# A long convolution and a SwiGLU on one core: another order of the steps in all five queues

## The chip, the cores and the metric

The kernel runs on one core of a Trainium2 chip. The metric is the device time of one execution in microseconds (us). Four engines compute: TensorE (PE, matmuls), VectorE (DVE), ScalarE (ACT) and GpSimd (POOL); SyncE (SP) issues nearly all transfers. Each engine works through its own list of instructions in order, and waits on semaphores where a step needs the result of another engine or of a transfer.

## The reference

For one sequence of S = 2048 rows with D = 640 channels in bf16 (F = 1728):

```python
def _A_ref(q, k, v, shift_k, ssm_k, ssm_D):       # q: a layernorm of A_q
    k_shift = sum over t of k_pad[:, t:t + S, :] * shift_k[:, ks - 1 - t]     # 4 taps
    kv = k_shift * v
    y_f = rfft(kv, padded to 2 S) * rfft(ssm_k, padded to 2 S)
    y = irfft(y_f)[:S] + kv * ssm_D
    return q * y

def _B_ref(x, w_gate, w_up, w_down):
    return (silu(x @ w_gate) * (x @ w_up)) @ w_down

x = A_q
h = x + _A_ref(_layernorm(x), A_k, A_v, A_shift_k, A_ssm_k, A_ssm_D)
h2 = h + _B_ref(_layernorm(h), B_w_gate, B_w_up, B_w_down)
```

(The first lines are shortened in their writing, not in what they compute.)

## The kernel before

**Blocks and stages.** The sequence is cut into four blocks of 512 rows, numbered 0 to 3. The long convolution is done block by block through a half-shifted discrete Fourier transform of 512 points, written as matmuls with a table of cosines and sines. The names below are those of the code, with i for the block:

- *k filter* (kt0 to kt3, kf0 to kf3). kc is the load of a block of ssm_k; kt transposes it on TensorE (line 538), ACT copies it to KT (L543); kf transforms it with the table ftab (matmuls L582, eviction to C and KO by ACT L595, butterflies by DVE L552), and DVE adds neighbouring blocks (L666). kf1 to kf3 each have eight matmul steps of four matmuls.
- *kv* (kv1 to kv3). kT is a transposing load of k's block (L484), of which PE makes the shifted sum of four taps (L686, L691) in three steps; ACT evicts them (L715; L698 in block 0); for blocks 1 to 3 five transposing transfers turn the result back into kvo (the "kvt pieces", L484), and three DVE products multiply v into it (L724, vt). In block 0 PE transposes back instead.
- *ln* (L784 to L813). Statistics and scaling of the gate, q; x is its load, L813 the scaling.
- *xf*, *p*, *iv*. The transform of kv, the products of block j's transform with the filter's (DVE, L753, L754, L759, L769), and the inverse transform with the table itab (PE, L830).
- *hn* (L850 to L889). DVE multiplies the inverse by q, ACT and POOL take the second LayerNorm's statistics, ACT scales (L886; in block 0 DVE, L889), and four transposing transfers per block, the "hn pieces", write hnT.
- *ff* (L911 to L988). Gate and up matmuls (L911, L912; L922 for the last half block), SiLU and copy on ACT (L934, L936), product on DVE (L938), down matmuls (L954, L966), eviction (ACT L974 with DVE L981; DVE L984 in block 3), and the store of the output (out, L988). Weights: GA, UA, GB, UB, PK, Wd.

**The order of work.** Every step is a task, numbered in the order in which the program creates it. `ORDER` is a table of these numbers, one list for each engine, and says in which order an engine's queue holds its tasks. `_Graph.schedule` replays the lists with a planner's costs. It assigns the accumulators (PSUM, four units of two banks each) in the order in which that replay reaches the tasks, so that a task also waits until the last users of its unit are done. It also counts filler: where the replay finds PE idle for more than 700 ns ahead of a step that opens a unit, `t.fill` throwaway matmuls of about 83 ns are put ahead of it (L249). `emit` then writes each engine's instructions with the waits that the dependences require.

```python
                if self.warm is not None and e == "pe" and at[e] > 2:
                    idle = s - max(free[e], unit_free[u])
                    t.fill = int((idle - 250) / 83) if idle > 700 else 0
```

Two helpers issue nearly all transfers: `load` (L479, a plain DMA) and `tload` (L484, a transposing DMA), both on SP except for a few loads at the start.

**The numbers used in the text.**

| queue | steps |
|---|---|
| SP | loads: 0 ident, 3 ftab, 4 itab, 17 kc0, 57 kc1, 62 kc2, 67 kc3; 19 v0, 314 v1, 507 v2, 710 v3; 138 x0, 312 x1, 505 x2, 708 x3; 225 UA, 224 GA, 227 UB, 226 GB, 228 and 229 PK, 230 to 233 Wd |
| SP | transposing: 18 kT0, 313 kT1, 506 kT2, 709 kT3; kvt1 317, 318, 321, 322, 325; kvt2 510, 511, 514, 515, 518; kvt3 713, 714, 717, 718, 721; hn0 202, 209, 216, 223; hn1 399, 408, 417, 426; hn2 602, 611, 620, 629; hn3 814, 823, 832, 841 |
| SP | stores: out0 298, 302, 307, 311; out1 491, 495, 500, 504; out2 694, 698, 703, 707; out3 905, 908, 912, 915 |
| PE | kt1 58, 60; kt2 63, 65; kt3 68, 70; kf1 72 to 86, kf2 94 to 108, kf3 114 to 128 (even numbers); kv1 315, 319, 323; kv2 508, 512, 516; kv3 711, 715, 719; iv0 192 to 195; ff0 from 238; ff1's down steps 486, 487, 488, 492, 496, 497, 501; ff2 from 630 |
| ACT | for a PE step n of kt, kf or kv, step n + 1 is its eviction (95 for 94, 123 for 122, 712, 716 and 720 for kv3); 156 to 159 the scaling in ln0; 198 an eviction of iv0; 619 the last scaling ahead of the hn2 pieces |
| DVE | 132 the first butterfly of kf3 that needs 123; 519 to 521 the products of kv2, 722 to 724 those of kv3; 777, 779 and 780 three steps in the products of the filter with blocks 1 and 2 (about 1.4, 1.4 and 0.7 us in the planner's costs) |

Of the kernel before, what the change touches and what calls it, by code (L numbers as in the profile page):

```python
# [58 lines left out]
class _Graph:  # L59
# [170 lines left out]
    def emit(self, block):  # L230
# [75 lines left out]

ORDER = {
    "pe": """
# [6 lines left out]
    """,  # L315
    "act": """
# [12 lines left out]
    """,  # L329
    "dve": """  # L330
# [10 lines left out]
    """,  # L341
    "pool": """
        5 10 6 8 7 9 11 153 197 218 204 200 211 221 207 214 338 423 405 396 414 531 626 608 599 617 734 838 820 829 811
    """,
    "sp": """
# [3 lines left out]
    """,  # L349
}  # L350

# [716 lines left out]
```

## Time and profile before

| | |
|---|---|
| median of 3 runs | 273.35 us (273.2 to 273.37) |
| span of the profiled execution | 269.5 us; its own time outside the span isn't recorded |
| median less span | 3.85 us |
| busy in the span: PE | 255.2 us (95%), 1643 instructions |
| busy in the span: DVE | 203.8 us (76%), 282 instructions |
| busy in the span: ACT | 206.9 us (77%), 394 instructions |
| busy in the span: POOL | 24.1 us (9%), 35 instructions |
| moved by DMA | 25.85 MB |

The span runs from the first to the last recorded instruction of one execution; the times are the device times of separate executions. Busy time counts an engine's instructions alone, so that issuing a DMA or waiting on a semaphore is idle time there. Several rows below come from views that group instructions: "x20" is the number in the group, and "[2.01 <-DMA kT]" at the end of a row says that the engine had been idle for 2.01 us before it and that a transfer into kT ended that.

### The profile page before, as it was taken

The page shows a single profiled execution, that of the slowest core. Times are in us where ns is not written, and L with a number is a line of the kernel's source. Part 1 is how long each engine was busy: PE and PEld are TensorE (multiplying, and loading weights), DVE is VectorE, ACT ScalarE, POOL GpSimd, SP SyncE. Part 2 cuts the span into 40 slices and gives each one's busy share as a digit, 9 for nine tenths or more (in the row PEclk, how much of TensorE's full clock was granted, in tenths as well). Part 3 has the DMA queues.
Part 4 walks back from the last instruction along what each step waited for, and adds up shares of the span by engine and source line. Part 5 has one row for each costly group of instructions (what it writes and reads, how often), then busy time and mean ns, then how long its engine had stood idle before and what let it go on. Part 6 is the DMA issues. An engine that isn't in the chain of part 4 may idle for free.

```text
span 269.5 us, 4198 instructions
## 1 busy us (share of the span) xinstructions
PE 255.2 (95%) x1643; PEld 144.2 (53%) x1660; DVE 203.8 (76%) x282; ACT 206.9 (77%) x394; POOL 24.1 (9%) x35
## 2 busy tenths in 40 slices
PE   7799797999999999999999997999999999999995
PEld 5576455545444666554446574454446674444663
DVE  2399999899999999999999998999996100042312
ACT  2799999797889999479969997399889963647400
POOL 0000315000030013000200141000200200000000
PEclk9999999999999999999999999999999999999999
DMA  6999909551173608643000336510000050010002
GB/s 124 373 355 369 340 19 124 112 138 73 30 261 122 103 0 103 135 155 100 0 1 16 86 63 119 129 80 1 2 0 0 2 122 0 2 49 0 0 27 99
DMA packets 42501, 25.85 MB, mean 96 GB/s; under 512 B 32241, under 2 KB 41202, under 8 KB 42482
## 3 DMA queue, kind: packets, MB, share of 16 engines
q1 hardware_dynamic: 41824, 25.58, 35.7%
q8 instruction: 13, 0.21, 0.3%
q10 hardware_dynamic: 658, 0.01, 0.1%
q14 instruction: 6, 0.05, 0.1%
HBM read 15.69 MB, written 2.62 MB: 68 GB/s over the span
## 4 chain that ended last, share of the span: by engine, by line
DVE 41%; PE 27%; ACT 19%; DMA 6%; SPq 3%; issue 2%; POOL 1%; DVEq 0%
PE ps L954 11%; DVE T L753 6%; DVE T L754 6%; PE ps L912 6%; PE ps L911 5%; DVE T L759 5%; DVE Y L769 5%; DVE gu L938 4%; DVE X L552 3%; SPq L484 3%; DMA kT<-in_A_k_dram 3%; ACT KT L543 3%; ACT KO L595 2%; DVE C L666 2%; DMA kc<-in_A_ssm_k_dram 2%
## 5 line engine op out<-in xcount | busy, mean ns | idle before, releaser
L954 PE MATMUL ps<-Wd,gu 128*128 128x384 bf16 (+1 forms) x416 | 59.0, 299 | 0.2 <-ACT qo L854 0.2
L912 PE MATMUL ps<-hnT,UA 128*128 128x512 bf16 x140 | 53.1, 379 | 0.5
L911 PE MATMUL ps<-hnT,GA 128*128 128x512 bf16 x132 | 50.0, 379 | 1.3 <-DMA hnT<-qo 1.3
L954 PEld LDWEIGHTS ps<-Wd,gu 128*128 128x128 bf16 x416 | 40.0, 98 | 18.3 <-issue 1.3
L936 ACT ACTIVATE ub<-ps 128x512 bf16<-128x512 f32 (+1 forms) x60 | 33.7, 568 | 18.5 <-PE ps L912 11.3
L912 PE MATMUL ps<-hnT,UB 128*128 128x512 bf16 x120 | 45.5, 379 | 0.2
L911 PE MATMUL ps<-hnT,GB 128*128 128x512 bf16 x117 | 44.3, 379 | 0.0
L938 DVE TENSOR_TENSOR gu<-gu,ub 128x512 bf16<-128x512 bf16 x52 | 21.5, 421 | 25.1 <-ACT ub L936 13.2
L934 ACT ACTIVATE gu<-ps 128x512 bf16<-128x512 f32 x52 | 29.8, 596 | 12.6 <-PE ps L912 12.4
L753 DVE TENSOR_TENSOR T<-X,C 128x2560 bf16<-128x2560 bf16 x20 | 29.7, 1486 | 0.2
L754 DVE TENSOR_TENSOR T<-X,C 128x2560 bf16<-128x2560 bf16 x20 | 29.7, 1486 | 0.1
L911 PEld LDWEIGHTS ps<-hnT,GA 128*128 128x128 bf16 x140 | 13.7, 98 | 18.2 <-DMA hnT<-qo 1.9
L582 PE MATMUL ps<-KT,ftab 128*128 128x320 bf16 x128 | 19.9, 300 | 2.5 <-ACT KT L543 1.8
L912 PEld LDWEIGHTS ps<-hnT,UA 128*128 128x128 bf16 x140 | 13.7, 98 | 15.7
L881 POOL TENSOR_TENSOR mv<-mv,half 128x1 f32<-128x1 f32 x16 | 13.7, 859 | 68.2 <-ACT mv L874 68.2
L911 PEld LDWEIGHTS ps<-hnT,GB 128*128 128x128 bf16 x120 | 11.7, 98 | 14.2 <-ACT ub L936 0.2
L759 DVE TENSOR_TENSOR T<-T 128x1280 bf16<-128x1280 bf16 x24 | 19.2, 819 | 0.1
L912 PEld LDWEIGHTS ps<-hnT,UB 128*128 128x128 bf16 x120 | 11.7, 98 | 14.0
L582 PE MATMUL ps<-vt,ftab 128*128 128x320 bf16 x128 | 19.0, 299 | 0.1
L804 POOL TENSOR_TENSOR st<-st,half 128x8 f32<-128x8 f32 x4 | 7.9, 1981 | 113.1 <-ACT st L798 113.1
L769 DVE TENSOR_TENSOR Y<-Y,T 128x2560 bf16<-128x2560 bf16 x12 | 17.8, 1484 | 0.0
L582 PEld LDWEIGHTS ps<-KT,ftab 128*128 128x128 bf16 x128 | 11.0, 98 | 10.7 <-ACT KT L543 3.1
(86 smaller groups left out, 376.5 us busy)
## 6 DMA issues: line engine op xcount, KB each, us to landing
kc<-in_A_ssm_k_dram SPq DMA_DIRECT2D x4, 640.0 KB, 10.1
vt<-in_A_v_dram SPq DMA_DIRECT2D x4, 640.0 KB, 4.8
xh<-in_A_q_dram SPq DMA_DIRECT2D x4, 640.0 KB, 5.9
out_dram<-xh SPq DMA_DIRECT2D x16, 160.0 KB, 2.0
Wd<-in_B_w_down_dram SPq DMA_DIRECT2D x1, 1280.0 KB, 7.5
UA<-in_B_w_up_dram SPq DMA_DIRECT2D x1, 1120.0 KB, 13.5
GA<-in_B_w_gate_dram SPq DMA_DIRECT2D x1, 1120.0 KB, 10.5
UB<-in_B_w_up_dram SPq DMA_DIRECT2D x1, 960.0 KB, 7.5
```

What stands on the lines that cost most here:

```text
L582: last = e.matmul(pt.f(c, W), ftab[:, cs, j, f * P:(f + 1) * P], src[:, j, c * W:(c + 1) * W], start=(j == par), stop=(j == par + 2))
L753: g.add("dve", nm, lambda e, x=x, k=k, t1=t1: e.tensor_tensor(out=t1, in0=x, in1=k, op=ALU.mult), cdve(2560), r=[x, k], w=[t1])
L754: g.add("dve", nm, lambda e, x=x, k=ksw, t2=t2: e.tensor_tensor(out=t2, in0=x, in1=k, op=ALU.mult), cdve(2560), r=[x, k], w=[t2])
L759: g.add("dve", nm, lambda e, p=p, q=q, d=d, op=op: e.tensor_tensor(out=d, in0=p, in1=q, op=op), cdve(1280), r=[p, q], w=[d])
L769: g.add("dve", nm, lambda e, y=y, z=z: e.tensor_tensor(out=y, in0=y, in1=z, op=ALU.add), cdve(2560), r=[y, z], w=[y])
L881: g.add("pool", nm, lambda e, m=m: e.tensor_tensor(out=m[:, 3:4], in0=m[:, 2:3], in1=half[:, 1, 0:1], op=ALU.pow), 650, r=[m[:, 2:3], half ...
L911: e.matmul(pt.f(0, N), wg[:, c, f0:f0 + P], hnT[:, c, :], start=(c == 0), stop=(c == NC5 - 1))
L912: last = e.matmul(pt.f(1, N), wu[:, c, f0:f0 + P], hnT[:, c, :], start=(c == 0), stop=(c == NC5 - 1))
L934: g.add("act", nm, lambda e, pt=pt, gv=gv, a=ps_g, ts=ts: e.activation(out=gv, in_=pt.f(a[0], N, a[1])[:, ts], func=ACTF.Silu, scale=gain) ...
L936: g.add("act", nm, lambda e, pt=pt, uv=uv, a=ps_u, ts=ts: e.activation(out=uv, in_=pt.f(a[0], N, a[1])[:, ts], func=ACTF.Copy, scale=gain) ...
L938: g.add("dve", nm, lambda e, uv=uv, gv=gv: e.tensor_tensor(out=gv, in0=gv, in1=uv, op=ALU.mult), cdve(n), r=[gv, uv], w=[gv])
L954: last = e.matmul(pt.flat(c1 - c0, P + c0), slots[fb][:, j * P:(j + 1) * P], Wd[:, fb, c0:c1], start=(fb == 0 and not second), stop=(fb == ...
```

## The change

All five lists of `ORDER` are replaced. Each holds the same tasks as before; no task is added, removed or altered, and nothing else in the program is touched. What follows from the lists, the units of PSUM, the waits and the filler, is worked out anew by `schedule` and `emit`. Cut to the parts spoken of in this document:

```diff
     "pe": """
-        13 20 24 32 22 35 26 28 39 47 43 37 41 30 51 45 49 170 162 164 166 160 60 172 58 168 174 82 72 80 65 70 63 86 74 68 78 120
-        118 84 124 116 114 128 76 192 193 195 194 126 108 96 319 122 104 315 323 94 102 98 100 106 238 234 246 349 351 357 347 345
...
+        13 20 24 32 22 35 26 28 39 47 43 37 41 30 51 45 49 170 162 160 164 166 60 168 70 172 58 174 65 78 118 76 120 80 68 84
+        82 74 86 114 63 72 124 116 192 195 193 194 108 98 128 94 102 315 319 96 126 122 323 100 106 104 238 234 246 351 347
...
-        439 548 540 538 546 544 542 550 552 431 443 447 451 455 467 463 459 471 475 479 593 591 590 592 486 711 487 488 715 496
-        492 497 719 501 630 638 634 754 762 748 752 758 760 750 756 642 650 646 658 662 654 666 682 670 674 678 805 803 689 804
+        308 516 435 427 439 548 540 538 546 544 542 552 550 431 443 451 447 463 459 455 467 475 471 479 593 591 592 590 486
+        719 715 487 488 496 492 497 711 501 630 638 634 762 752 748 750 754 756 758 642 760 646 662 650 654 658 666 682 674
...
     "act": """
-        85 119 117 125 129 156 157 115 159 158 198 77 199 219 220 205 212 206 213 109 97 127 320 105 123 316 324 103 99 329 95 101
+        75 87 115 64 85 73 125 156 159 157 117 158 198 219 199 205 220 129 206 212 95 99 109 213 316 320 103 97 123 127 101
...
-        465 536 473 469 472 476 535 477 480 481 621 603 534 623 605 483 594 624 484 625 606 612 712 627 607 596 614 597 609 598
-        610 615 628 489 600 616 601 716 618 619 498 720 493 502 632 631 640 639 635 755 636 763 749 759 753 725 761 751 726 757
+        530 461 460 464 456 457 535 536 468 469 465 537 477 534 476 473 480 621 472 603 623 624 594 481 625 612 484 596 597 627
+        483 614 720 598 605 615 716 616 600 606 628 607 489 618 601 609 610 619 493 712 502 498 632 631 639 640 636 763 635
...
     "dve": """
-        186 187 154 188 189 155 191 184 190 90 196 91 130 217 203 210 88 201 131 222 89 208 93 215 92 132 366 365 368 367 327 370
+        186 184 188 187 185 189 154 191 155 190 88 196 90 217 203 130 210 89 201 91 222 92 208 131 215 93 366 365 368 367 327
+        132 328 241 370 326 110 372 369 249 111 361 371 112 362 133 237 374 373 113 375 376 245 363 257 253 364 377 340 380
...
-        746 595 485 747 613 768 770 769 773 771 775 772 490 774 778 499 494 776 724 777 723 503 779 633 722 780 781 783 782 641
+        474 744 604 743 482 595 745 613 746 485 768 747 770 769 773 771 775 772 490 774 778 494 776 780 777 499 779 503 633
+        722 723 724 781 783 782 637 785 784 641 764 786 645 787 765 766 649 788 789 790 767 791 795 653 792 657 661 796 735
...
     "pool": """
-        5 10 6 8 7 9 11 153 197 218 204 200 211 221 207 214 338 423 405 396 414 531 626 608 599 617 734 838 820 829 811
+        5 8 10 9 11 6 7 153 197 218 204 200 211 221 207 214 338 423 405 396 414 531 626 599 617 608 734 838 820 829 811
     "sp": """
-        0 18 17 19 3 138 4 57 225 228 67 62 312 314 232 227 229 224 233 313 202 223 209 216 322 318 325 321 317 226 507 230 231
-        506 426 511 510 408 399 417 514 302 515 518 307 298 311 505 710 709 714 611 713 629 602 491 620 718 500 717 495 721 504
-        708 841 823 832 814 703 698 694 905 908 912 707 915
+        0 18 17 19 3 138 62 229 57 67 232 227 4 228 312 225 224 314 313 202 223 209 216 322 318 317 325 321 226 230 233 231
+        506 426 510 408 399 417 507 511 515 518 514 298 307 302 311 505 709 718 710 629 602 611 620 717 713 714 721 491 504
+        500 495 708 841 823 832 814 698 703 707 912 908 905 694 915
```

38 rows, old and new, of the table ORDER are left out of this document.

## The prediction

> **What bounds the kernel now.** First the head of the page and the table of stretches, whose columns after the stretch's length are the busy time of TensorE (PE), its weight loads (PEld), VectorE (DVE), ScalarE (ACT) and GpSimd (POOL).
>
> ```profile
> span 269.5 us, 4198 instructions
> PE 255.2 (95%) x1643; PEld 144.2 (53%) x1660; DVE 203.8 (76%) x282; ACT 206.9 (77%) x394; POOL 24.1 (9%) x35
> q8 instruction: 13, 0.21, 0.3%
> DVE 41%; PE 27%; ACT 19%; DMA 6%; SPq 3%; issue 2%; POOL 1%; DVEq 0%
> ...
> 13.70:41.00 27.30, 24.93 (x210) 16.33 (x208) 26.66 (x43) 27.22 (x41) 3.07 (x2) 1.00 0.80 264
> 60.00:167.00 107.00, 105.67 (x660) 58.53 (x667) 105.95 (x136) 93.64 (x187) 12.94 (x10) 1.00 0.35 88
> 169.00:204.00 35.00, 34.84 (x178) 17.34 (x180) 34.70 (x45) 28.75 (x57) 1.78 (x1) 1.00 0.13 40
> 204.00:266.30 62.30, 61.92 (x375) 35.26 (x376) 13.77 (x30) 33.26 (x69) 2.20 (x4) 1.00 0.11 30
> ```
>
> PE is busy 95% of the span, yet the chain that ended last runs more through DVE. The table says why. From 13.7 to 41 us ACT is full (27.22 of 27.30). From 60 to 167 and from 169 to 204 DVE and PE are both full, and after 204 PE alone. So there is little to win inside the long stretches; what an order can win are the holes between them. Second, the holes themselves, in the timelines of PE and of DVE; the bracket at the end of a row is the idle time before it and who ended it.
>
> ```profile
> 43.85 1.81 PE L249 MATMUL ps<-ident 128*128 128x192 bf16 x20
> 47.67 1.06 PE L691 MATMUL ps<-kT,dg 64*64 64x512 bf16 x16 [2.01 <-DMA kT<-in_A_k_dram]
> 162.86 0.81 PE L686 MATMUL ps<-kT,dl 128*128 128x512 bf16 x3 [0.61 <-ACT kT L715]
> 168.53 0.39 PE L911 MATMUL ps<-hnT,GA 128*128 128x512 bf16 x1 [1.33 <-DMA hnT<-qo]
> ...
> 46.76 0.45 DVE L889 TENSOR_SCALAR qo<-xh,mv 128x640 bf16<-128x640 bf16 x1 [0.44 <-POOL mv L881]
> 51.29 0.83 DVE L552 TENSOR_TENSOR C<-C,KO 128x1280 bf16<-128x1280 bf16 x1 [0.81 <-ACT C L595]
> 58.72 0.42 DVE L938 TENSOR_TENSOR gu<-gu,ub 128x512 bf16<-128x512 bf16 x1 [0.47 <-ACT ub L936]
> 168.95 0.43 DVE L724 TENSOR_TENSOR vt<-vt,kvo 128x512 bf16<-128x512 bf16 x1 [1.67 <-issue]
> ```
>
> There are two places. Around 44 to 48 us PE does 1.81 us of filler (L249) and waits another 2.01 for kT1, the transposing load of k's second block. Around 167 us PE waits 1.33 us for hnT, the last transposed piece of the third block, and DVE 1.67 us for a product of kv3, whose releaser the profile can't name. Both wait for transposing transfers. Third, then, the transfers in short stretches: the last number of a row is the time from issue to landing, and the GB/s line cuts its stretch, here 40.6 to 47.7 us, in 40 slices of 0.18 us. The five transfer rows below it are of stretches from 40, 146, 164, 214.5 and 165.2 us, the last two of one from 168.
>
> ```profile
> GB/s 0 0 0 0 0 0 0 42 153 131 221 147 185 281 275 274 294 284 293 332 275 271 215 62 10 7 9 48 161 173 190 192 136 13 7 9 9 10 50 112
> ...
> q8 instruction: 1, 0.02, 0.9%
> q14 instruction: 1, 0.01, 0.4%
> ...
> kT<-in_A_k_dram SPq DMA_TRANSPOSE x1, 7.0
> ...
> kT<-in_A_k_dram SPq DMA_TRANSPOSE x1, 4.8
> ...
> hnT<-qo SPq DMA_TRANSPOSE x1, 4.4
> ...
> hnT<-qo SPq DMA_TRANSPOSE x4, 2.6
> ...
> kvo<-kT SPq DMA_TRANSPOSE x1, 3.5
> ...
> out_dram<-xh SPq DMA_DIRECT2D x1, 160.0 KB, 2.0
> kvo<-kT SPq DMA_TRANSPOSE x1, 2.4
> ```
>
> kT1 (40.6) took 7.0 us where kT3 (146.2) took 4.8; the hnT piece that PE waits for (164.1) took 4.4 where the four from 214.9 took 2.6; the kvo piece that DVE waits for (165.4) took 3.5, one at 168.4 took 2.4. In kT1's stretch the packets all but stop twice, for about 0.7 us each, and just two instruction fetches fall into it, one on PE's queue (q8) and one on q14. So a fetch costs transposing transfers in flight some 1 to 2 us. This is what the change goes for.
>
> **Part 1, the start (13 to 60 us).** Every queue holds the same steps in another order, so engine time stays and only waits (and PE's filler) can change. ACT is full from 13.7 to 41 and exchanges steps of equal cost, so step 156, the first LayerNorm scaling, comes at about 37.1 as before: no gain there. UB's load (227) now stands sixth after x0 on SP. It waits until kc1 has been transposed (step 58, by its place at about 23.5 us), and itab, PK, x1, UA, GA, v1 and kT1 wait behind it.
>
> ```profile
> GB/s 124 373 355 369 340 19 124 112 138 73 30 261 122 103 0 103 135 155 100 0 1 16 86 63 119 129 80 1 2 0 0 2 122 0 2 49 0 0 27 99
> ...
> vt<-in_A_v_dram SPq DMA_DIRECT2D x1, 640.0 KB, 4.0
> ```
>
> At the page's 360 GB/s or so (second to fifth slice) these 5.2 MB take 14.4 us; a load by itself takes 4.0 for 640 KB, so about 2.2 before its data. They end near 23.6 + 2.2 + 14.4 = 40.2; itab, first needed near 37, lands by 31. kT1's first packet comes 1.2 us after its issue (the seven empty slices above), so near 41.3: the queue costs nothing, at most 0.9 us if loads run slower.
>
> kT1 needs the third product of iv0. One kf3 step (128) moves from before iv0 to behind it.
>
> ```profile
> 51.72 2.88 PE L582 MATMUL ps<-KT,ftab 128*128 128x320 bf16 x20
> 54.44 0.38 PE L911 MATMUL ps<-hnT,GA 128*128 128x512 bf16 x1
> 38.09 2.49 PE L830 MATMUL ps<-IO,itab 128*128 128x320 bf16 x16
> ```
>
> Twenty such matmuls take 2.72 us from start to start, four (one step) 0.54. The third product now ends at 40.58; DVE's part before it keeps its length, so I take 0.45 of the 0.54 and issue kT1 at 40.15. It lands at 45.0 with 4.8, at 47.15 with 7.0. Five k-filter steps (108, 98, 128, 94, 102) instead of three stand before kv1, whose PSUM pair is freed by ACT's step 95. ACT ran a nearly equal list, from 198 to before 109, between these two starts:
>
> ```profile
> 40.99 1.02 ACT L850 ACTIVATE qo<-xh,mv 128x640 bf16<-128x640 bf16 x1
> 45.91 0.68 ACT L595 ACTIVATE KO<-ps 128x640 bf16<-128x640 f32 x1
> ```
>
> With 95 in place of a small step that is about 46.1. PE starts kv1 at 46.1 (clean) or 47.15 (hit) with one step more done than now: 47.67 − 46.1 + 0.54 = 2.1 us ahead, or 1.1. What is late next is DVE, full from here on. Its three holes sum to 1.72: the 0.81 goes, since step 132 (it waits for ACT's 123) now stands behind five others; the other two shrink as kv1 and ff0 come sooner. I take **−1.3 us**, bounds −0.5 and −1.7.
>
> **Part 2, v2's load (100 to 117 us).** Step 507 leaves its place near 72 us, where nothing waited for it, and goes between the last hn1 piece and four kvt2 pieces on SP. DVE's product 519 needs those.
>
> ```profile
> 104.19 4.42 SPq L484 DMA_TRANSPOSE hnT<-qo  x3
> ...
> 115.58 0.95 DVE L724 TENSOR_TENSOR vt<-vt,kvo 128x1536 bf16<-128x1536 bf16 x1
> ...
> L484 SPq DMA_TRANSPOSE kvo<-kT x15: 1188/1267/2357, 50.5 to 170.3; - x15
> ```
>
> hn1's issues end at 108.61, 1.3 earlier then at 107.3. A piece takes 1.27 to issue (median). If the pieces overlap with the load, the last is issued at 107.65 + 3 × 1.27 = 111.5 and lands by 113.9; if they move only after it has landed (107.3 + 4.0), at 111.3 + 4 × 1.27 = 116.4. DVE wants them at 115.58 − 1.3 = 114.3. Bounds 0 and +2.1; no transposing piece of the trace stands behind a load in flight. I take **+0.5**, nearer to the row with the 2.4, reached right after a store of 160 KB.
>
> The Trainium skill, page "DMA: Bandwidth & Descriptors", section "Two DMAs through the same engine are not ordered", says that descriptors of one queue start in order. By that alone +2.1 would stand here; no run shows it yet.
>
> **Part 3, the third block (146 to 175 us).** On SP the four hn2 pieces now stand together with kvt3 behind them, but for 718, and v3's load before them, with over 2 us to spare; on ACT kv3's short eviction (720) comes ahead of LayerNorm's last scaling (619) in place of a long one (712); on DVE the kv3 products (722 to 724) stand behind 780, 777 and 779.
>
> ```profile
> 161.57 1.01 ACT L715 ACTIVATE kT<-ps 128x1024 bf16<-128x1024 f32 x1
> 162.86 0.29 ACT L884 ACTIVATE mv<-mv 128x1 f32<-128x1 f32 x1 [0.28 <-POOL mv L881]
> 164.69 0.58 ACT L715 ACTIVATE kT<-ps 128x512 bf16<-128x512 f32 x1
> 172.84 0.42 DVE L938 TENSOR_TENSOR gu<-gu,ub 128x512 bf16<-128x512 bf16 x1
> ```
>
> 619 ends 0.43 + 0.28 earlier. With Part 1's 1.3 and a turn in SP's queue its transfer is issued near 163.0 and lands at 165.6 clean, when PE gets there: PE's 1.33 goes, and most of its 0.61. The kvt3 pieces follow at 1.27: the last is issued at 168.0, landing at 170.4, or 171.8 if hit. DVE gets to 722 at 173.26 − 1.3 − 1.67 = 170.3, as 780 (0.75) comes in ahead and two products (0.7) go out. So 0.1 to 1.5 of wait replaces 1.67: I take 0.4, hence **−1.3 us**, bounds −0.2 and −1.6. From 169 to 204 DVE is full and then PE to the end, so this arrives at the end as long as ff2 starts 2.1 us sooner, by 166.4.
>
> **The sum.** −1.3 + 0.5 − 1.3 = −2.1 us on a span of 269.5. The median of the runs is 273.35, 3.85 above the span; that part lies outside the first and last instruction and is taken as unchanged: **271.3 us**, the forecast's own range 270.4 to 272.4.
>
> **The rivals.** *Everything clean* (chance 0.11): −1.7, 0 and −1.6 make −3.3, 270.0. Against it: the fetches on q14 keep their places in programs whose length is the same.
>
> *Fetches only move* (0.10), so that the change does not do what it says: PE's filler may shrink from 20 matmuls, which shifts every later fetch of PE against the transfers. With kT1 hit (−0.5 for −1.3) hn2's last piece is issued at 163.0 + 0.8 + 0.5 = 164.3; hit too, it lands 4.4 later at 168.7, PE starts ff2 there instead of at 168.53 and is full from then on: 273.5.
>
> *Slower: v2's load holds the kvt2 pieces* (0.24). Its place is 107 to 117 us, and it decides once the last piece lands after 114.3: DVE stops, and with it all that follows. With the full +2.1, kT1 hit (−0.5) and kvt3 nearly so (−0.3) it makes +1.3: 274.6. For it: one queue carries load and pieces. Against: three issues take 3.8 us anyway, about as long as the load.
>
> *Fetches cost nothing* (0.09): the long landings come from the burst of pieces itself and stay. kT1 at 7.0 leaves −0.5; hn2's last piece, issued at 163.8, lands with 4.4 at 168.2, and PE, full from there, gains 0.3: 273.0. Against it stand the two stops with one fetch each.
>
> The Trainium skill, page "Runtime: NRT & Kernel Launch", section "Instruction fetch mechanics", calls the cost of crossing a 16 KiB block of instructions mostly hidden; by that this last rival would hold. The trace agrees on the block (13 fetches, 0.21 MB) but has transfers 1.1 to 2.2 us longer beside them.
>
> **How the numbers follow.** The forecast has 0.46. A measurement of this kernel tells 0.2% (0.55 us) from no change, so faster means below 272.8 and slower above 273.9. Faster: 0.45 of the forecast, 0.11 of the clean case, 0.02 of the moved fetches and 0.03 of the last, 0.61. Slower: 0.24 and 0.02 of the moved fetches, 0.26. The rest, 0.13, lies within. The range goes from just below the clean case to the slower one: 269.9 to 274.6.
>
> **What would show it.** Right: kT1 lands in about 5 us and kv1 starts by 46.6; step 132 no longer stops DVE; 519 starts by 115; PE's wait near 165 is under 0.3. Wrong: kT1 again near 7; DVE idle over 1 us between 107 and 117 until kvo comes; a new wait of PE for kT2 near 93 or for hnT near 109; holes of PE after 204.

## The result, and the profile after

The median went from 273.27 us (4 runs) to 270.12 us (4 runs, 269.86 to 270.2): a ratio of 0.9893, with a 95% interval of 0.9861 to 0.9925, so 1.1% or 3.15 us faster. The forecast was 271.3, so 2.05 us faster. The profiled executions differ by less: spans of 269.5 and 267.7 us. Four single runs far outside all others (990.53 us and twice about 1516 us of the kernel before, 385.44 us of the one with 40 fillers) are left out of every count and median below. The head of the page of the changed kernel, busy time by engine and the chain that ended last:

```profile
span 267.7 us, 4177 instructions
PE 255.2 (95%) x1640; PEld 141.7 (53%) x1640; DVE 203.6 (76%) x282; ACT 206.5 (77%) x394; POOL 22.5 (8%) x35
PE 33%; DVE 30%; ACT 26%; DMA 5%; SPq 3%; issue 2%; DVEq 0%
```

PE now has the largest share of the chain, where DVE had it before. (The text of `ORDER` is one line longer, so every line of the program behind it has moved by one: L692 is L691 before.) Next the two places where PE and DVE waited, in the timelines of PE and of DVE; the bracket is the idle time before a row and what ended it.

```profile
44.55 0.72 PE L583 MATMUL ps<-KT,ftab 128*128 128x320 bf16 x4 [0.61 <-ACT KO L596]
46.13 1.92 PE L692 MATMUL ps<-kT,dg 64*64 64x512 bf16 x32 [0.86 <-ACT C L596]
...
162.58 3.71 PE L955 MATMUL ps<-Wd,gu 128*128 128x384 bf16 x26
166.12 0.38 PE L912 MATMUL ps<-hnT,GA 128*128 128x512 bf16 x1
...
173.12 1.12 PE L583 MATMUL ps<-vt,ftab 128*128 128x320 bf16 x7 [0.36 <-DVE vt L725]
```

```profile
48.48 0.45 DVE L890 TENSOR_SCALAR qo<-xh,mv 128x640 bf16<-128x640 bf16 x1 [0.52 <-POOL mv L882]
...
54.98 0.82 DVE L553 TENSOR_TENSOR C<-C,KO 128x1280 bf16<-128x1280 bf16 x1
...
58.20 0.96 DVE L725 TENSOR_TENSOR vt<-vt,kvo 128x1536 bf16<-128x1536 bf16 x1 [0.22 <-DMA kvo<-kT]
...
113.93 1.62 DVE L725 TENSOR_TENSOR vt<-vt,kvo 128x512 bf16<-128x512 bf16 x3
...
171.43 1.63 DVE L725 TENSOR_TENSOR vt<-vt,kvo 128x1536 bf16<-128x1536 bf16 x3 [0.26 <-DMA kvo<-kT]
```

The filler (L249) is gone, since the planner found no long enough gap. PE starts kv1 at 46.13 instead of 47.67 and no longer waits for kT1, but 0.86 us for an accumulator that ACT still evicts. Step 132 (54.98) waits for nothing. At 166.12 PE takes up ff2 without a wait, 2.41 us earlier than before, and DVE's wait near 167 has shrunk from 1.67 to 0.26. New is PE's 0.36 at 173.12: xf3 needs a kv3 product. Last, transfers issued in three short stretches (40 to 46, 107 to 115 and 162.9 to 172 us), with the median time from issue to landing at the end of a row:

```profile
kT<-in_A_k_dram SPq DMA_TRANSPOSE x1, 5.6
...
vt<-in_A_v_dram SPq DMA_DIRECT2D x1, 640.0 KB, 4.5
out_dram<-xh SPq DMA_DIRECT2D x4, 160.0 KB, 1.9
kvo<-kT SPq DMA_TRANSPOSE x4, 3.4
...
kvo<-kT SPq DMA_TRANSPOSE x4, 2.8
hnT<-qo SPq DMA_TRANSPOSE x2, 2.7
```

kT1 takes 5.6 us instead of 7.0, and the last hn2 pieces 2.7 instead of 4.4. The instruction fetches near them are at 47.7 and 167.6 us, where before they were at 45.6 and 166.1: out of kT1 and hn2, into the hn0 pieces and the kvt3 pieces.

### The profile page after: what moved, and what is told of

Read it like the earlier page. It is cut to its first block, busy times and chain, and to the rows that moved or that the text cites. A ratio compares the mean times of both kernels' runs of the same rounds, so it can differ in the third digit from the quotient of the medians.

```text
span 267.7 us, 4177 instructions
## 1 busy us (share of the span) xinstructions
PE 255.2 (95%) x1640; PEld 141.7 (53%) x1640; DVE 203.6 (76%) x282; ACT 206.5 (77%) x394; POOL 22.5 (8%) x35
## 4 chain that ended last, share of the span: by engine, by line
PE 33%; DVE 30%; ACT 26%; DMA 5%; SPq 3%; issue 2%; DVEq 0%
PE ps L955 16%; DVE T L754 5%; PE ps L912 5%; PE ps L913 5%; DVE Y L770 4%; DVE T L760 4%; DVE T L755 4%; DVE gu L939 4%; DVE X L553 3%; ACT KO L596 3%; SPq L485 3%; DMA kvo<-kT 3%; PE ps L831 3%; ACT KT L544 3%; ACT C L596 2%; ACT xh L814 2%
## 5 line engine op out<-in xcount | busy, mean ns | idle before, releaser
L912 PE MATMUL ps<-hnT,GA 128*128 128x512 bf16 x140 | 53.1, 379 | 0.0
L912 PE MATMUL ps<-hnT,GB 128*128 128x512 bf16 x120 | 45.5, 379 | 0.0
L912 PEld LDWEIGHTS ps<-hnT,GA 128*128 128x128 bf16 x140 | 13.7, 98 | 16.2 <-ACT FO L596 0.2
L912 PEld LDWEIGHTS ps<-hnT,GB 128*128 128x128 bf16 x120 | 11.7, 98 | 14.5 <-ACT ub L937 0.4
L805 POOL TENSOR_TENSOR st<-st,half 128x8 f32<-128x8 f32 x4 | 8.6, 2139 | 116.5 <-ACT st L799 116.5
L882 POOL TENSOR_TENSOR mv<-mv,half 128x1 f32<-128x1 f32 x16 | 11.0, 688 | 68.3 <-ACT mv L875 68.3
```

What stands on the lines that cost most here:

```text
L912: e.matmul(pt.f(0, N), wg[:, c, f0:f0 + P], hnT[:, c, :], start=(c == 0), stop=(c == NC5 - 1))
```

## The experiments

Two theories stood at the start. F: instruction fetches hold up transposing transfers, and the change wins by where its fetches fall. O: the order alone wins, and the fetches are incidental. A third question came from the times: 273.35 us stood 3.85 above the span of before, but 270.12 only 2.4 above 267.7.

**The kernel before, again.**

> The kernel before, unchanged. What lies outside the span was 3.85 us in the numbers of before (273.35 against 269.5), but 2.1 to 2.2 us in all four runs of the changed kernel. Theory A: about 2.2 us lie outside in every run, and the profiled execution of before was a short one; its runs then have spans of 271.0 to 271.3, and a new profile shows where the 1.5 us more come in (a longer kT1, hn2 or kvt3 transfer, since those are the waits of PE and DVE). Theory B: before has 3.85 us outside the span; the spans are 269.4 to 269.6 at 273.3 us.

Neither theory fits whole. The time lies 1.8 to 2.2 us above the span in every run, as A says. But the runs fall into two groups, which the granted clock tells apart: nine at 0.998 to 1.000 (271.33 to 272.29 us) and three at 0.992 to 0.994 (273.17 to 273.35). The profile caught one of the three (span 271.2 us). Its slices of the clock, then the table of stretches behind the wait for kT1 (the column after POOL is the granted clock), then PE's timeline:

```profile
PEclk9999999799999999999999999999999999999999
```

```profile
47.50:48.00 0.50, 0.50 (x12) 0.30 (x16) 0.50 (x1) 0.01 (x1) 0.00 (x0) 0.97 0.87 171
48.00:49.00 1.00, 1.00 (x13) 0.19 (x6) 0.96 (x3) 0.00 (x0) 0.00 (x0) 0.50 0.52 100
49.00:50.00 1.00, 1.00 (x5) 0.54 (x6) 1.00 (x1) 0.98 (x1) 0.00 (x0) 0.50 0.73 142
50.00:51.00 1.00, 1.00 (x5) 0.41 (x3) 0.23 (x1) 0.04 (x1) 0.00 (x0) 0.50 0.81 161
51.00:51.50 0.50, 0.50 (x9) 0.20 (x12) 0.00 (x0) 0.24 (x1) 0.00 (x0) 0.62 0.04 7
```

```profile
47.48 1.49 PE L691 MATMUL ps<-kT,dg 64*64 64x512 bf16 x16 [2.08 <-DMA kT<-in_A_k_dram]
48.91 2.32 PE L582 MATMUL ps<-KT,ftab 128*128 128x320 bf16 x8
```

PE waits 2.08 us for kT1, starts kv1, and from 48.0 to 51.4 us it runs at half its clock. Eight matmuls that take 1.26 us at full clock take 2.32. The transfer itself took 7.1 us, as before. In all, 31 of the 88 clocked runs of before carry such a dip, and cost some 1.7 us more (medians 273.67, 273.49 and 273.73 against 272.02, 271.86 and 271.87 in the three comparisons). So the profile in the prediction shows a run without the dip, while three of the first four times have the level of runs with it (their clock isn't on record). Below, "clean" means runs at a granted clock of 0.998 or more.

**Without filler.**

> The kernel before in its own order, without the 20 filler matmuls ahead of kv1: every later instruction fetch of PE comes 40 instructions later, the first of them behind kT1's landing (at about 49 in place of 45.6), the one near 166 behind hn2's last piece. Theory F (fetches cost the transposing transfers in flight 1 to 2 us): kT1 lands in 5.6 us or less, hn2's last piece in about 2.7, PE's 2.01 and 1.33 shrink to under 1 and under 0.5; time 1.0 to 2.0 us under before. Rival O (the order alone counts; the long landings come of what stands beside them in the queue): kT1 again near 7, hn2's last piece near 4.4, time within 0.3 us of before. Filler gone also lets PE idle for 4 us: if its granted clock fell from 1.00, PE would be slower behind it.

```diff
-                    t.fill = int((idle - 250) / 83) if idle > 700 else 0
+                    t.fill = 0
```

PE's timeline, and the transfers issued between 40.3 and 46.1 and between 163.3 and 166.7 us:

```profile
46.12 1.06 PE L691 MATMUL ps<-kT,dg 64*64 64x512 bf16 x16 [2.40 <-DMA kT<-in_A_k_dram]
...
166.31 0.38 PE L911 MATMUL ps<-hnT,GA 128*128 128x512 bf16 x1
```

```profile
kT<-in_A_k_dram SPq DMA_TRANSPOSE x1, 5.7
...
hnT<-qo SPq DMA_TRANSPOSE x1, 2.6
```

Not one step of the order differs from before; only the fetches come 40 instructions later (47.6 and 167.8 us). kT1 lands in 5.7 us, the last hn2 piece in 2.6, PE has no wait at 166, and the clean runs are at 270.02 us: 2.0 under before, as low as the changed kernel. That is theory F, at the upper end of what it expected, and rival O falls. But 8 of the 12 runs have the dip (median 271.61), so the median is only 271.48, ratio 0.9963 (0.9934 to 0.9991). The wait that the page shows as 2.40 was 2.01 with 1.81 of filler ahead of it, and without filler the clock gives way more often.

**The start alone.**

> All five queues in the changed order up to about 60 us of the span, then in the order of before. This is Part 1 of the prediction by itself: -1.3 us, bounds -0.5 and -1.7, if the third block's waits stay (PE 1.33, DVE 1.67 near 167). Its plan has no filler either, so the later fetches move as in the run without filler; theory F adds up to 1.0 us of gain there (together -1.3 to -2.5), rival O doesn't (-0.5 to -1.7).

```diff
     "sp": """
-        0 18 17 19 3 138 4 57 225 228 67 62 312 314 232 227 229 224 233 313 ...
+        0 18 17 19 3 138 62 229 57 67 232 227 4 228 312 225 224 314 313 ...
```

All five lists follow the changed order, as this one does, for steps that start before 60 us, and the order of before from there. Clean runs are at 270.57 us, 1.45 under before; over all, the ratio is 0.9949 (0.9926 to 0.9972). The profile caught a run with the dip, so its times behind kv1 are some 1.5 us late. kT1 took 5.6 us, kv1 started as in the changed kernel, hn2's last piece took 2.6 us, and PE took up ff2 without a wait, although the third block has the order of before: its fetches have moved too (107.3 and 168.9 us). So the gain of the start can't be split in this run between order and fetches, and it doesn't reach the -2.5 that F allowed. Four of 12 runs had the dip.

**The third block alone, twice.**

> All five queues in the order of before up to 145 us, then in the changed order: Part 3 by itself, with the filler and the fetches of before. The prediction: -1.3 us, bounds -0.2 and -1.6; PE's wait for hnT near 167 under 0.4, DVE's for kvo under 1. Theory F: the fetch at 166 now falls into the kvt3 pieces, which then land up to 1.6 us late, and DVE waits for them at 722 to 724 (gain under 1). Rival O: no such wait, gain of 1.3 or more.

> The third block alone once more (the order of before up to 145 us, the changed order behind it), now with DVE's short pauses, which the planner counts anew for every order, where the changed kernel has them. In the first try one POOL step of the second LayerNorm took 5.0 us in place of 0.65 beside a run of wide DVE products without a pause, and ACT waited 2.5 us for it. If the pauses are the cause: that step takes under 1.3 us, the scalings come as in the changed kernel, and the time in clean runs goes from 274.1 to 271.0 (0.9 under before; bounds 270.3 and 271.8, by what the fetch near 168 now hits). If the changed order of the third block by itself holds POOL up: again about 274.

```diff
+        for t in g.tasks:
+            t.pause = g.tasks[PAUSE[t.seq]] if t.seq in PAUSE else None
```

The lists follow before up to 145 us and the changed order from there; the lines above are those of the second run. `PAUSE` has DVE's pauses (a wait for its own last step) where the changed kernel has them. POOL's timeline, first run and then second (L879 is L881 before):

```profile
156.04 5.87 POOL L879 TENSOR_TENSOR mv<-mv,half 128x1 f32<-128x1 f32 x2 [4.01 <-ACT mv L872]
163.27 0.78 POOL L879 TENSOR_TENSOR mv<-mv,half 128x1 f32<-128x1 f32 x1 [1.36 <-ACT mv L872]
```

```profile
156.25 0.79 POOL L879 TENSOR_TENSOR mv<-mv,half 128x1 f32<-128x1 f32 x1 [4.02 <-ACT mv L872]
158.87 1.04 POOL L879 TENSOR_TENSOR mv<-mv,half 128x1 f32<-128x1 f32 x1 [1.84 <-ACT mv L872]
```

The first was 274.13 in clean runs (two; the other four had the dip), ratio 1.0105 (1.0061 to 1.015), for a reason neither theory had: of the two POOL steps in the first row, one took 5.0 us beside a row of wide DVE products. With the pauses back the two take 0.79 and 1.04, and the clean median is 271.70 us (nine runs, 270.85 to 272.97). That is 0.16 under before, where the prediction's Part 3 had 1.3 and this expectation 0.9. The transfers issued between 166 and 171.3 us say what was hit:

```profile
q8 instruction: 1, 0.02, 1.1%
...
kvo<-kT SPq DMA_TRANSPOSE x4, 3.0
hnT<-qo SPq DMA_TRANSPOSE x1, 2.6
```

hn2's last piece is clean here, by the order alone. The fetch of PE, at 168.3, falls into the kvt3 pieces behind it. Two landed 4.5 and 3.5 us after issue, yet DVE waited only 0.26 for kvo and PE 0.36 for the product. Of the 1.03 us that this order wins between 143 us and ff2's start (PE's last gate and up step of ff1 comes 0.61 later than before, ff2's first L912 0.42 earlier, at 168.34), 0.36 is left at the end: the rest is lost again within ff2, as in the changed kernel.

**v2's load early.**

> The changed kernel with v2's load back at its early place on SP. Part 2 of the prediction put +0.5 us (0 to +2.1) on its new place. The profile after shows the first kvt2 piece behind it landing 0.7 us after the load and the three others within 1.8 more, and DVE without a wait there: the price is 0, and this run is within 0.3 us of the changed kernel. By the +0.5 it would be 0.5 us faster.

```diff
-... 226 230 233 231 506 426 510 408 399 417 507 511 ...
+... 226 507 230 233 231 506 426 510 408 399 417 511 ...
```

Clean runs 270.23 (ten) against 270.35 (eight) of the changed kernel beside it: the place of this load is worth 0.1 us or nothing.

**Fetches moved into the transfers.**

> The changed kernel in its own order, with PE's instruction fetches moved some 76 instructions earlier: the warm-up at the start has 50 short matmuls in place of 24 long ones, and 12 filler matmuls stand in PE's wait for kc0. The fetch that came at 47.7 then comes near 44, inside kT1's transfer; one near 162 falls among the hn2 pieces. Theory F (fetches hold up transposing transfers): kT1 takes 6.5 to 7.2 us in place of 5.6, PE starts kv1 0.5 to 1.1 us later, hn2's last piece lands 0.5 to 1 later; 0.7 to 2.0 us over the changed kernel in clean runs. Rival O (only the order counts): within 0.3 us of it.

```diff
-                for k in range(WARM):
-                    last = e.matmul(pt.f(k % 2, N // 2), z[:, 0:P], z, start=True, stop=True)
+                for k in range(50):
+                    last = e.matmul(pt.f(k % 2, 64), z[:, 0:P], z[:, 0:64], start=True, stop=True)
...
+        g.tasks[32].fill = 12
```

Half of it missed. The fetch came at 41.4 us, ahead of kT1's data, and kT1 took 5.5. And the other warm-up cost something itself: the profiled run has PE at half its clock from 7.5 to 10.9 us, behind a wait of 2.69, and reaches kv1 1.1 us later. Later fetches hit, at 150.1 and 164.5 us. PE's timeline, then hn2 pieces issued in a stretch of 3.2 us, here (from 161) and, the last row, in the changed kernel (from 160):

```profile
152.66 0.81 PE L687 MATMUL ps<-kT,dl 128*128 128x512 bf16 x3 [1.74 <-DMA kT<-in_A_k_dram]
...
168.23 0.38 PE L913 MATMUL ps<-hnT,UA 128*128 128x512 bf16 x1 [0.30 <-DMA hnT<-qo]
```

```profile
hnT<-qo SPq DMA_TRANSPOSE x3, 4.7
```

```profile
hnT<-qo SPq DMA_TRANSPOSE x3, 2.8
```

kT3 took 6.3 us instead of 4.9, and PE waited some 1.5 us for it (the row's 1.74 takes in a matmul that has no record, as the step's weights were loaded from 152.43 on; the second row's 0.30 is too long in the same way). The hn2 pieces took 4.7 instead of 2.8. PE stood 0.86 us behind the changed kernel ahead of these and 1.89 at ff2; 1.36 arrived at the end. Clean runs are at 271.88, 1.5 over the changed kernel; with the start's share in it, the part of the fetches in those runs is not settled by this run alone.

**The wait filled up.**

> The kernel before with 40 filler matmuls ahead of kv1 in place of 20: they take 1.66 us more of PE's 2.01 us of wait for kT1, so that PE is idle for 0.2 to 0.6 us there. Its instruction fetches come 40 instructions earlier, the first of them still within kT1's transfer, so that the clean runs stay near 271.9 us (271.2 to 272.6). So far 24 of 71 runs of before had the granted clock near 0.993 and were 1.7 us longer, 8 of 12 without filler, and 2 of 14 of the changed kernel, which idles 0.86 us there. Theory C (the dip of the clock follows PE's idle time ahead of kv1): at most 1 run of 12 with a dip. Rival D (dips come whatever PE does there): 3 or more of 12.

```diff
         g.schedule(ORDER)
+        g.tasks[319].fill = 40
```

```profile
43.82 3.46 PE L249 MATMUL ps<-ident 128*128 128x192 bf16 x40
47.54 1.06 PE L691 MATMUL ps<-kT,dg 64*64 64x512 bf16 x16 [0.25 <-DMA kT<-in_A_k_dram]
```

PE idles 0.25 us, kT1 is as late as before (6.9 us), and no run has the dip: eleven of eleven at 0.998 or more, with a median of 271.43, while 7 of 17 runs of before beside it dipped. Theory C holds. A later fetch, now at 150.7 us, falls into kT3, which takes 6.5 us instead of 4.8: theory F in the other direction, in the old order. The ratio is 0.9959 (0.9934 to 0.9985): 20 more throwaway matmuls make the old order faster.

**The changed kernel again, and a variant.**

> The changed kernel, unchanged, in twelve more runs. So far the runs of before fall in two groups: granted clock 0.998 to 1.000 with 271.2 to 272.3 us, and 0.992 to 0.994 with 272.7 to 274.1; the profile of such a run has PE at half its clock for 3.4 us right behind its wait for kT1. Theory C (the dip follows that wait, and the change has taken the wait away): all or nearly all runs at 0.998 or more, 269.8 to 270.3 us, so that the difference to before is 1.7 us in clean runs and about 3.2 against the runs with a dip. Rival D (dips come by chance wherever): a quarter or more of the runs at 0.992 to 0.994 and about 271.8 us.

> The changed kernel once more, beside the two others on the same chip: clean runs at 270.1 to 270.4 us, and a dip of the clock in at most 3 of 12.

> The changed kernel with v2's load early and, on DVE, the kv3 product 722 behind 723 and 724: 722 alone needs the last kvt3 piece, for which DVE waits 0.26 us, and PE then 0.36 for the product, in the profile after. If that wait is what xf3 starts late by, 0.2 to 0.4 us under the changed kernel in clean runs (about 270.0); if it is not on the path to the end, the same within 0.15.

The changed kernel had 8 clean runs of 10 (270.35 us) and 6 of 6 (270.20); ratios 0.9916 (0.989 to 0.9942) and 0.99 (0.9861 to 0.9939). With the first four it dipped in 2 of 20 runs: few, as theory C has it, but not none: PE still idles there in three short holes, 1.92 us in all.

```diff
-        722 723 724 781 ...
+        723 724 722 781 ...
```

The variant, with 507 early and DVE's products in the order 723 724 722, has 269.84 us (six runs, 269.45 to 270.81), ratio 0.9889 (0.9853 to 0.9925). Its own profile doesn't show the reason that was expected: DVE's wait has moved behind the two products and kept its size, and PE's has kept its own (0.37). In DVE's timeline L722 is L724 before:

```profile
171.34 0.75 DVE L722 TENSOR_TENSOR vt<-vt,kvo 128x512 bf16<-128x512 bf16 x2
172.35 0.96 DVE L722 TENSOR_TENSOR vt<-vt,kvo 128x1536 bf16<-128x1536 bf16 x1 [0.26 <-DMA kvo<-kT]
```

So 0.36 us in overlapping ranges is not a shown gain; that it is clear of before is.

| kernel | clean runs, median us | runs with the dip |
|---|---|---|
| before, beside three groups | 272.02, 271.86, 271.87 | 28 of 76 (with its own run again: 31 of 88) |
| before without filler | 270.02 | 8 of 12 |
| before, filler 40 | 271.43 | 0 of 11 |
| start alone | 270.57 | 4 of 12 |
| third block alone, first run | 274.13 | 4 of 6 |
| third block alone, pauses kept | 271.70 | 3 of 12 |
| changed | 270.12, 270.35, 270.20 | 2 of 20 |
| changed, v2 early | 270.23 | 2 of 12 |
| changed, fetches moved (in the profiled run the dip is at 7.5 us) | 271.88 | 6 of 12 |
| changed, v2 early, 722 last | 269.84 | 0 of 6 |

## Why the prediction was right, and where not

The direction, the range and most steps held; the sum came out about right for the clean runs and too small for the median, and two of its terms were wrong by themselves.

*What bounds the kernel* held: fetches cost transposing transfers 1 to 2 us. The run without filler shows it without any change of order (7.0 to 5.7 and 4.4 to 2.6 us), and 2.0 us of time with it. The section "Instruction fetch mechanics" of the Trainium skill's page "Runtime: NRT & Kernel Launch" calls the cost of crossing a block of instructions mostly hidden. Here 40 instructions of shift moved the clean runs by 2.0 us, so beside transposing transfers it isn't, and the measurement decides.

*Part 1* (-1.3; bounds -0.5 and -1.7) was right step by step as far as kv1. kT1 was issued at 40.08 (forecast 40.15) and landed at 45.65, between 45.0 and 47.15: only the small fetch at 44.3 was left in it. ACT's step 95 ended at 46.08 (46.1), PE started kv1 at 46.13 (46.1), and 132 no longer stopped DVE. The other two holes, which were to shrink, didn't quite: 0.52 for a mv of POOL (0.44 before) and 0.22 for kvo are left, 0.74 of 1.72, so that DVE comes to step 519 only 0.98 us earlier, still between the bounds. The start alone gave -1.45 in clean runs, with what its moved fetches gave in it.

*Part 2* (+0.5, up to +2.1) was mis-sized: it measured 0.1 or nothing. v2's load landed at 111.62, and the first kvt2 piece behind it at 112.32, so it was held, as the upper bound had it. The step that failed is the one after: the bound let the four pieces follow each other at 1.27 us, the time of an issue, but pieces that have been issued already landed within 1.8 us in all. DVE came to its product at 114.60 without a wait. With it falls the slower rival that had this load for its mechanism.

*Part 3* (-1.3) was right at its place and wrong at the end. hn2's last piece was issued at 163.07 (forecast near 163.0) and landed at 165.70 (165.6); PE's 1.33 went, and ff2 started 2.41 us earlier than before, from 1.02 ahead of the third block. DVE waited 0.26 (0.4). The run without filler took up ff2 at 166.31 with the old order of the third block, so the gain at this place doesn't need the new one. (Of the 0.61 ahead of kv3 that the prediction also counted, some 0.2 is a matmul without a record: the row has three of four, and the step's weights were loaded from 162.63 on.) What failed is "this arrives at the end as long as ff2 starts 2.1 us sooner, by 166.4". It started at 166.12, and 0.66 was given back by the end, 0.36 of it in PE's new wait for a kv3 product, which the change had put behind three other steps on DVE. PE gets there 2.4 us earlier, but DVE ends its kv3 products only 1.2 us earlier (at 173.06 instead of 174.25). The trace of the third block alone agrees, with its clean gain of 0.16.

In the profiled executions the sum was -1.75 (DVE's last step ends at 265.44 instead of 267.20), where the prediction had -2.1. PE was 1.02 ahead at the third block, where Parts 1 and 2 make 0.8, and Part 3 brought 0.73 in place of 1.3: that the sum came out near is luck, two misses of opposite sign.

*The sum against the median* failed: 3.85 us above the span was "taken as unchanged". What lies outside the span is 1.8 to 2.2 us. The other 1.7 were, by the level of the times, the dip of the clock, in the runs that made the median and not in the run that was profiled. The changed kernel is without it in 18 of 20 runs. So of the 3.15 us, 1.5 to 1.9 is seen in clean runs (271.86 to 270.35 and 271.87 to 270.20 side by side, 272.02 to 270.12 across two groups), and the rest comes of the mix of runs: three of the first four of before have the level of the dip, where 31 of 88 carry it. It is by this chance that the median lies on the rival "everything clean" (270.0) and not on the forecast. v2's load did cost nothing, as that rival has it, but its -3.3 stands against -1.75 in the profiles. A granted clock of 0.998 beside a median 1.7 us too high was there to be asked about.

*"Fetches only move"* was a rival with 0.10, priced at 273.5 for a filler that shrinks. The filler did go, and the fetches did move, but out of the transfers that PE waited for. By the run without filler, that alone is worth as much in clean runs (four of them, 270.02) as the whole change; that the order gains anything of its own in clean runs is not shown. Theory F is shown, in one direction cleanly. What the order adds is that it has other work to do ahead of kv1, so that PE idles in three short holes (0.45, 0.61 and 0.86 us) and not in one of 2.4, and the dip comes more rarely.

## What to carry to other kernels

Compare the time of the profiled run with the median of the others before using its span, and look at the granted clock to three digits: a profile can be of the other kind of run. When an order is changed, count what moves besides the steps: filler, instruction fetches and pauses moved here, and one of them alone was worth 2 us. A stall that ends sooner is worth what the next wait leaves of it, so follow it to the next product that the freed engine needs.

## What the runs showed of the hardware

- An instruction fetch of PE (16 KB) holds up transposing transfers in flight. In the 13 traces kT1 to kT3 took 4.7 to 5.2 us with no fetch beside them, 4.7 to 5.6 with PE's at their very start or end, 5.5 to 5.9 with the 8 KB one on q14, 6.3 to 6.5 with PE's alone some 4 us after their issue, 6.8 to 7.1 with both. Of the 403 hn and kvt pieces 103 took over 3.05 us; beside 80 of them a fetch of PE was in flight, ahead of the other 23 a load.
- After a wait of PE ahead of kv1 the granted clock fell to 0.50 for 3.4 us, in a share of the runs that followed the idle time there: 8 of 12 for 2.4 us, 31 of 88 for 2.0 behind filler, 8 of 50 with the changed start, 0 of 11 for 0.25. The Trainium skill, page "TensorE: Matmul & The Clock Gate", section "What's actually happening", has half clock after an idle window of about 3.4 us and says that the windows run freely. The traces agree on the windows, but a wait of 2.0 us was enough. In the 11 traces with a record of the clock, its full stretch begins at 3.9 to 7.0 us of the span, and the clock changes only at whole multiples of 3.413 us behind that (all three dips at kv1 at 40.96, twelve windows). PE's idle time, summed by these windows up to 266 us, is 1.8 to 2.4 us in the four that a dip follows and at most 1.77 in any other. So short holes in one window add up, somewhat over half a window is enough, and where the grid falls over the wait decides which runs are hit.
- A POOL step that takes some 0.65 us took 5.0 beside a row of wide DVE products without a pause, and 1.04 with one pause among them. The Trainium skill, page "SBUF — State Buffer", section "SBUF: two separate sides", calls the port that the two share an exclusive lock; the trace agrees with the effect.
- Transposing transfers held back behind a load land 0.5 to 0.75 us apart, where 1.27 us lie between their issues.
